# Thirteen weight parts split on other engines, ten of them by GpSimd's scaling and subtraction, with a new order of all jobs and of the memory part's bank reads

## The chip, the cores and the metric

The kernel runs on one core of a Trainium2 chip. The metric is the device time of one execution in microseconds (us), the median of several runs. TensorE (PE) multiplies matrices, VectorE (DVE) and ScalarE (ACT) read its results from PSUM, GpSimd (POOL) works in SBUF alone, and SyncE (SP) issues nearly all DMAs.

## What is computed

The input x has 2048 tokens of 512 numbers. After a layer norm it goes two ways, and the results are added to x:

```python
xn = _layernorm(x)
return x + _A_ref(xn, wq, wk, wv, wo, beta) + _B_ref(xn, w1, b1, w2, b2)

# _A_ref: 32 heads of 16, four segments s of 512 tokens, for each head
p = softmax(q_s @ k_s.T * scale + mask)        # mask adds -1e9 where key > query
a_dot = p @ v_s
a_mem = (phi(q_s) @ M) / (phi(q_s) @ z + 1e-6)
o = g * a_mem + (1 - g) * a_dot                # then o @ wo over all heads
M, z = M + phi(k_s).T @ v_s, z + sum(phi(k_s)) # memory for the next segment

# _B_ref: a second layer norm y of xn, then
h = gelu(y @ w1 + b1)                          # 1792 hidden numbers
out = h @ w2 + b2
```

## The kernel before

**Numbers in two halves.** A float32 operand of a large product is held as two float16 tiles, a high part h and a rest l, and a product takes three matmuls (hh, hl, lh; `split3`, line 482). So every weight matrix is loaded, scaled by a power of two, and split. A matrix is cut into parts (`PARTS`, line 42) and each part into pieces of 128x512. For a part there are loads (`w_load`, SP's DMAs), squares for the scale (`w_square`, line 290; for the parts in `TRACES` four or more small matmuls and a DVE reduction), the scale itself (`w_scale`, line 341: one small matmul job, two ACT and some small DVE instructions), and one split job for each piece (`w_split`, line 364).

**Three ways to split.** The letters of `SPLIT` (line 45) choose one for each piece:

```python
if SPLIT[m][n] == "P":
    G.tensor_scalar(h, r, s, 0.0, op0=OP.mult, op1=OP.add)                 # L371
    V.scalar_tensor_tensor(l, r, s, h, op0=OP.mult, op1=OP.subtract)      # L372
elif SPLIT[m][n] == "V":
    A.activation(h, r, AF.Copy, scale=s)                                   # L374
    V.scalar_tensor_tensor(l, r, s, h, op0=OP.mult, op1=OP.subtract)      # L375
else:                                                                      # "G"
    G.tensor_scalar(r, r, s, 0.0, op0=OP.mult, op1=OP.add)                 # L377
    A.activation(h, r, AF.Copy)                                            # L378
    G.tensor_tensor(l, r, h, op=OP.subtract)                               # L379
```

In all three the three instructions (two for P and V) follow one another.

**Jobs and their order.** The work is cut into 1308 jobs in 41 streams (`streams`, line 55). Attention goes by 16 units i (segment s = i // 4, eight heads each): `T` projects queries (which = 0) or keys (1), sends them to DRAM and fetches them back in another layout (`qk_proj`, line 513; L527 to L529 write, L535 reads), `M` makes scores for the row maxima (`m_jobs`, PE L637, DVE L644), `R` turns the maxima and puts them beside the queries (PE L507, SP L659), `S` makes scores again and takes exponentials (PE L676, ACT L681, POOL L690), `pv` and `PV` multiply with the values (PE L705), `O` normalizes. `N` and `K` update the memory, `Z`, `Qd` and `Q` read it. The MLP goes by 16 half blocks j: `D` (PE L488, DVE L771), `G` (GELU on ACT), `H` (split of the hidden tile by POOL, ACT, POOL) and `e` (PE L812). `V` projects values, `out` the attention result (PE L830). 14 jobs `warm` (`warm_up`, line 838) are fillers: eight matmuls of ones whose result nobody reads.

`ORDER` (line 98) is a string written out by hand or by a planner: each letter names a stream and takes its next job, and that is the order in which every engine's instructions are issued. An engine works through its own instructions strictly in that order. `BANKS` (line 115) gives, in the same order, which of the eight PSUM banks each result takes; a job whose bank is still being read waits on PE. Nothing else sets the order.

**The memory part.** `a_mem` (line 571), part 0, is the job `Qd` of units 4 to 15: two matmuls (PE L579) fill two banks; ACT copies the denominators (L585) and DVE scales the numerators (L588), each from both banks, one half of the partitions from each. In the kernel before ACT begins with the first bank and DVE with the second, and then they change over.

Of the kernel before, what the change touches and what calls it, by code (L numbers as in the profile page):

```python
# [57 lines left out]
def streams():  # L58
# [40 lines left out]
    "aufauucvafauaxuEdwuxEGayFEbayuFGEaaGuAeGzEzFGguHHGJHufFiHAHHhHIJIHpHpJHGIpHJFIppppIjjIBqjBqBgIJKoItIqKKoKujjjCC"  # L99
    "hIKLjqjjLoLoDJKjajrrjnKrrqLrjijtrJjpKpKJLJkrkkpkjrKjrtjkpJpkjrtjKKjltlllpjkrLjkpkjkrjrLLkkgjLllLntqllhppqLrkLDk"  # L100
    "mpupqmkktkmpppjkrrMjjllqlljkrqrjkrrirjkrkjkMarMrjkghpjqrjrajrjqlllnlijrqmqppjjMpqpkjmkpkkjpkjrararmkjrjrrjjtraq"
    "nlallalujrkrrkjrkrbjrarMkappqkjkhqglqlllkkpmpapMkkimppkrkrmjjlllljrjrqkjrrjkrjrkjrkjrMrjkrnkrrqjqjllllMmmogojnm"
    "hsnsoktakkspkqjjkotkjjnlllljjkspqnkkjpkjrkrjrjkrjajllllqrjmrmigprknmhpkkrrtkrkkppnllllnkkrjrnrkrkkpjikpqjjjlltq"
    "llpmpqmpgppjnjqhrqrqrjrrrjrqjrrjjpqpjtrjrjqjrmtpjrnkrkppjkkpkjjpkjaqallllnjakrtrkrarkkrrjakrinrjkrjtllllbarrjam"
    "mpgpkrkrrkmnkkhppknllllnakkupkknpijkkjpqjjlqllljmjojmjgonjjqhqojjmoqjssqjkkskjrkkrrjjrrjtklnlllnkjrrnkjrkrktjrk"
    "rjrkqjrjqjllllsijmqrmpgpkknhkkqpmppkkrpllnllnrjkrjrkjrrkjtritjrkjrrjkpkjrjrqrjqqrjjllllmpnmpgtpjnqhqppppnkrkrrk"
    "rkrrrtakrjrjrqqjarrjrjrjppppmtkjjtqjpppjaaqllllnjjrkqrrkrkaarkrajrirnkrkraallllbrkmrmkgkrkrknkhmpplnlnnllkkpppk"
    "kjpkjkqpjjjlllljqjqoqjjojmjjmgojmnhosnkkkqssnkjksjjklllljrkrjrkrjrkjrkjrkrkrjrjtjrtqqjllllrjrmrmgnhpkpqppnnkkkk"
# [8 lines left out]
    "605426105420416520146502415602415602410526410263502741650713264350174305174304157305417305417340751340751430154"
    "730261275403621750436217450362170362170362170136127306132706312703241567025374167405231670421653704653704653704"
    "653764057364507367540367021365463670241536704521367014352675240136713542067134250675130675301765361075173605361"
    "057317603517670351672504317632054135764021753647021532641253645215364215346213675042103564271063541273065421370"  # L120
    "653470653476053647054367054673056470532617405613247670153026754213064752163045721634514620751342641073526410472"
    "351460723460273436027342607342067342607432607432672017453614270536451270616234561543261542361542361542316542632"
    "154637405216327153406271523147513247513247516324105763245137062451306742513052041352041352054130254130125436026"
    "715430275402631752140635721046213756024137560243561702435726017265410372651403472651304651304651304650134650131"
    "436450173247126503472176350421763504271643276143726143712643712643723164507253106472053161304725163047521463701"
    "643701643701643701734036731430673410675212150627510627615032607"
# [799 lines left out]
```

## Time and profile before

| | us |
|---|---|
| median of 3 runs | 688.02 |
| lowest and highest | 687.28, 688.51 |
| the profiled execution, its own time | 687.96 |
| its span, first to last instruction | 686.3 |

A profile gives each engine's instructions with start and duration. A row of a timeline merges neighbours: start, length, engine, line, operation, tiles, form, count (x12 is twelve instructions), and in brackets the idle time of the engine before it and what ended it. PEld is the weight load that goes beside a matmul; SPq is the issuing of a DMA. Matmuls are pipelined and the ends in the records are modelled, so the length of a merged row is longer than the distance to the next one's start; where a price of a PE job is wanted, that distance is used.

### The profile page before, as it was taken

How to read it: one execution, taken by the hardware profiler on the slowest of the kernel's cores; microseconds unless marked ns; L12 is line 12 of the kernel's file. 1: busy time of each engine (PE TensorE's matmuls, PEld its weight loads, DVE VectorE, ACT ScalarE, POOL GpSimd, SP SyncE). 2: the span in 40 equal slices, each digit the busy share in tenths (PEclk: the TensorE clock that was granted, in tenths of full speed). 3: DMA queues.
4: the chain of work that ended last, by engine and by line, in shares of the span. 5: the costliest groups of instructions: out<-in, count | busy, mean ns of one | idle time of the engine just before them, and what ended most of it. 6: DMA issues, size and time to landing. Idle time of an engine off the chain costs nothing.

```text
span 686.3 us, 17241 instructions
## 1 busy us (share of the span) xinstructions
PE 677.1 (99%) x6465; PEld 389.1 (57%) x6465; DVE 542.6 (79%) x1740; ACT 502.6 (73%) x972; POOL 339.4 (49%) x526
## 2 busy tenths in 40 slices
PE   8999999999999999999999999999999999999997
PEld 6755656565644556565554556557564446556643
DVE  6999977997897867898687886979678697959532
ACT  4585798788785668667796857775875686877970
POOL 4445567446543444564435454445444335565652
PEclk9999999999999999999999999999999999999999
DMA  9886132320305113222123123151020415240101
GB/s 277 258 227 196 47 83 75 94 48 15 112 3 154 32 55 72 65 60 63 58 69 108 34 71 85 32 126 47 17 79 25 116 18 154 33 108 3 19 1 63
DMA packets 52433, 54.89 MB, mean 80 GB/s; under 512 B 5486, under 2 KB 41340, under 8 KB 52348
## 3 DMA queue, kind: packets, MB, share of 16 engines
q1 hardware_dynamic: 50044, 49.59, 25.2%
q0 software_dynamic: 2304, 4.20, 3.8%
q8 instruction: 51, 0.84, 0.5%
q14 instruction: 34, 0.28, 0.1%
HBM read 36.72 MB, written 16.78 MB: 78 GB/s over the span
## 4 chain that ended last, share of the span: by engine, by line
PE 89%; DVE 4%; DMA 3%; ACT 2%; issue 1%; SPq 0%; POOL 0%; ACTq 0%; DVEq 0%
PE ps L488 37%; PE ps L812 20%; PE ps L705 10%; PE ps L830 6%; PE ps L676 5%; PE ps L637 5%; DVE ps L644 2%; PE ps L579 2%; ACT pt L681 1%; PE ps L507 1%; DMA wvs<-in_A_wv_dram 1%; PE ps L843 1%; PE ps L618 1%; PE ps L314 1%; DMA qst<-qd 1%
## 5 line engine op out<-in xcount | busy, mean ns | idle before, releaser
L644 DVE CUSTOM_DVE_ANT_0 ps<-ps,mask 128x512 f32<-128x512 f32 (+3 forms) x512 | 234.2, 523 | 12.9 <-PE ps L637 9.6
L681 ACT ACTIVATE pt<-ps,qkcs 128x512 f32<-128x512 f32 (+1 forms) x384 | 206.8, 625 | 31.8 <-PE ps L676 30.2
L812 PE MATMUL ps<-w2s,hT 64*128 64x512 f16 x1344 | 173.3, 375 | 0.1
L488 PE MATMUL ps<-xnT,w1s 128*128 128x256 f16 x1344 | 157.7, 273 | 0.3
L690 POOL TENSOR_SCALAR_AFFINE_SELECT pt<-pt 128x256 f32<-128x256 f32 x256 | 100.8, 421 | 89.3 <-ACT pt L681 88.1
L488 PEld LDWEIGHTS <-w1s 128*128 128x128 f16 x1344 | 128.0, 98 | 28.3 <-issue 10.3
L787 POOL TENSOR_TENSOR hT<-hh,hT 128x512 f16<-128x512 f32 x64 | 67.5, 1054 | 91.3 <-ACT hT L786 88.3
L812 PEld LDWEIGHTS <-hT 64*128 64x128 f16 x1344 | 68.3, 94 | 56.4 <-issue 2.9
L705 PE MATMUL ps<-pt,vt 128*32 128x512 f32 (+3 forms) x1024 | 76.0, 435 | 0.0
L771 DVE SCALAR_TENSOR_TENSOR hT<-ps,sc,sr 128x256 f32<-128x256 f32 x112 | 51.8, 478 | 24.9 <-PE ps L488 24.0
L644 DVE DVE_READ_ACCUMULATOR2_ANT mc<- 128x1 f32 x512 | 71.4, 139 | 0.1
L676 PE MATMUL ps<-qst,kst 50*128 50x512 f16 (+3 forms) x512 | 63.8, 298 | 0.8 <-ACT pt L681 0.7
L637 PE MATMUL ps<-kst,qst 48*128 48x256 f16 (+3 forms) x512 | 63.0, 297 | 0.5 <-DVE mc L644 0.2
L786 ACT ACTIVATE hT<-hh 128x512 f16<-128x512 f32 x64 | 36.6, 573 | 32.4 <-POOL hh L785 32.1
L705 PEld LDWEIGHTS ps<-pt,vt 128*32 128x32 f32 x1024 | 31.2, 109 | 41.0 <-issue 32.5
L785 POOL TENSOR_SCALAR hh<-hT,sc 128x512 f32<-128x512 f32 x64 | 41.7, 652 | 21.0 <-ACT hT L778 18.6
L778 ACT ACTIVATE hT<-hT,b1t 128x256 f32<-128x256 f32 x112 | 46.7, 496 | 1.1 <-DVE hT L771 0.8
L735 POOL TENSOR_TENSOR nN<-nN,oT 128x512 f32<-128x512 f32 x16 | 20.3, 1271 | 48.4 <-DVE oT L554 48.4
L488 PE MATMUL ps<-xnT,wqs 128*128 128x512 f16 x192 | 44.2, 380 | 0.0
L488 PE MATMUL ps<-xnT,wks 128*128 128x512 f16 x192 | 44.1, 379 | 0.0
L488 PE MATMUL ps<-wvs,xnT 128*128 128x512 f16 x192 | 43.8, 379 | 0.1
L830 PE MATMUL ps<-wos,oT 128*128 128x512 f16 x192 | 43.3, 379 | 0.0
(225 smaller groups left out, 873.5 us busy)
## 6 DMA issues: line engine op xcount, KB each, us to landing
kd<-hl SPq DMA_DIRECT2D x48, 128.0 KB
qd<-hl SPq DMA_DIRECT2D x48, 128.0 KB
kst<-kd SPq DMA_DIRECT2D x32, 192.0 KB
qst<-qd SPq DMA_DIRECT2D x32, 192.0 KB
acc<-in_A_x_dram SPq DMA_DIRECT2D x16, 256.0 KB
acc<-in_B_b_dram POOLq DMA_DIRECT2D x16, 256.0 KB, 4.2
out_dram<-acc SPq DMA_DIRECT2D x16, 256.0 KB
xt<-in_A_x_dram SPq DMA_DIRECT2D x14, 256.0 KB
```

Source lines behind the costliest of these rows:

```text
L488: T.matmul(p, wsl(ws, k, a), xsl(xs, k, b), start=s0 and i == 0, stop=s1 and i == 3 * n - 1)
L637: T.matmul(p[:, o:o + n], stk[i, 0][r, t, P * qb:P * qb + P], stk[i, 1][r, t, :n], start=True, stop=True)
L644: V.tensor_tensor_reduce(p[:, o:o + n], p[:, o:o + n], mask[:, 512 - n:], 1.0, -3e38, OP.add, OP.max, mc[:, 16 * b + 4 * t + qb:16 * b + 4 ...
L676: T.matmul(p[:, o:o + n], stk[i, 1][r, t, P * kb:P * kb + P], stk[i, 0][r, t, P * kb:], start=True, stop=True)
L681: A.activation(e[:, OFF[kbs[0]]:OFF[kbs[0]] + o], p[:, :o], AF.Exp, scale=qkcs[:, 1, i % NG:i % NG + 1])
L690: G.affine_select(v, v, pattern=[[0, 2], [1, P]], compare_op=OP.is_ge, fill=0.0, base=0, channel_multiplier=-1)
L705: T.matmul(p[32 * c:32 * c + 32, P * kb:], vt[s, kb][:, 4 * g + c, 16 * odd:16 * odd + 32], pt[i, 2 * c + odd][:, OFF[kb]:OFF[kb] + LEN[kb ...
L771: V.scalar_tensor_tensor(hz[:, fi, :], p[:, :256], col(F1 + fh), srow[hs][:, own], op0=OP.mult, op1=OP.mult)
L778: A.activation(z, z, AF.Gelu_apprx_tanh, bias=b1t[:, FH * (j % 2) + f:FH * (j % 2) + f + 1])
L787: G.tensor_tensor(hT[:, z, 1, :], t, hT[:, z, 0, :], op=OP.subtract)
L812: w = T.matmul(pes[j][a], hTs[fh][r, fi, u, P * a:P * a + P], w2s[r, fo, v, :], start=n == 0 and m == 0, stop=fi == FH - 1 and m == 2, ski ...
L830: T.matmul(p, o[:, u, P * b:P * b + P], wos[:, g, v, :], start=i == 0, stop=i == 3 * NG - 1)
```

## The change

`SPLIT` changes for 13 pieces of five parts: ten go to G (six from V, four from P), three go from P to V. The order of all 1308 jobs and the bank of each of the 1173 results are new. In `a_mem` both engines now take the first bank, then the second.

```diff
-SPLIT = {"qk": "VV", "QK": "PV", "RK": "PPPP", "v": "VPVP", "1a": "PVPVPVP", "2a": "PVPVPVP", "1b": "GVGVGVG", "2b": "GVGVGVG",
+SPLIT = {"qk": "GV", "QK": "GG", "RK": "PPPP", "v": "GVGP", "1a": "PVGVPGV", "2a": "GVGVPGV", "1b": "GVGVGVG", "2b": "GVGVGVG",
          "o": "GVGV"}
...
 ORDER = (
-    "aufauauucvafauaxuEdwuxEGayFEbayuFGEaaGuAeGzEzFGguHHGJHufFiHAHHhHIJIHpHpJHGIpHJFIppppIjjIBqjBqBgIJKoItIqKKoKujjjCC"
+    "ufucuuaavffxaxawuEdauuyEuGGyEaGzEauzFFaauGFGeAbEGguFHHAGHuIHHHhIJHHppJHJpHIHpppBFpJqIiBjjIIojjIKICtBoKqjjjJgKIh"
...
 BANKS = (
-    "307127514306527014705325621740356523475160172345670124345762013561047235612043715620415642015625401642501654201"
+    "301204250617342570316274261543270437614205043746125036754120637541650237146275031462751462756152746512746512754"
...
-            lo, hi = slice(0, 64), slice(64, 128)
-
-            def den(p, r, z):
+            for b, p in enumerate(ps):
+                r, z = slice(64 * b, 64 * b + 64), slice(64 - 64 * b, 128 - 64 * b)
                 A.activation(rd[r], p[z], AF.Copy, bias=1e-6, scale=qkcs[r, 0, g:g + 1])
-
-            def num(p, r):
                 V.tensor_scalar(n[r], p[r], bg[r, g, 4:5], None, op0=OP.mult)
-
-            den(ps[0], lo, hi)
-            num(ps[1], hi)
-            den(ps[1], hi, lo)
-            num(ps[0], lo)
```

The strings decode to these differences around which the prediction argues. The number in brackets is the job's place in the order, before and after.

```text
fillers                before: 1 4 5 11 14 18 29 36 46 52 105 224 340 693
                       after:  0 2 4 5 16 20 21 24 34 40 50 57 341 700
first traces, before:  warm, k(15), warm, q(20), v0(21), transpose, QK0(24) ... v1(31)
first traces, after:   warm, k(17), warm, warm, q(23), warm, v0(25), v1(26) ... QK0(36)
loads, before:         qk, v0, small, QK, v1, 1a, 1a, RK, 2a, 2a, RK
loads, after:          qk, v0, v1, QK, small, 1a, 1a, 2a, 2a, RK, RK
N of unit 0            before 55 (ahead of the first query projection, 60); after 85 (behind it, 62)
PE between T and M     unit 8:  before 4 D, 5 S, pv to PV, K, N, one filler; after the same without the filler
                       unit 14: before 7 D, 6 S; after 5 D, 4 S, pv to PV
                       unit 15: before 5 D, 4 S, pv to PV; after 5 D, 3 S, pv to PV
PE between R and S     unit 14: before two e, D, T; after PV, D, T
PE between the first   unit 15: before one S, one e; after one S, two e
S and the third S
PE between M and R     unit 15: before pv to PV; after pv to PV and one e
```

The number of changes between jobs that use 128 rows of the array and jobs that use 64 is 210 in both orders, and so is every other count of jobs the same.

## Rows read from the trace of the kernel before

**Rows 1.** The page, part 1: busy time, share of the span, instructions of each engine.
```profile
PE 677.1 (99%) x6465; PEld 389.1 (57%) x6465; DVE 542.6 (79%) x1740; ACT 502.6 (73%) x972; POOL 339.4 (49%) x526
```
**Rows 2.** The page, part 4: chain that ended last, share of the span by engine.
```profile
PE 89%; DVE 4%; DMA 3%; ACT 2%; issue 1%; SPq 0%; POOL 0%; ACTq 0%; DVEq 0%
```
**Rows 3.** Busy time by stretch: length, PE, PEld, DVE, ACT, POOL, PEclk, DMA share, GB/s.
```profile
0.00:60.00 60.00, 56.89 (x469) 39.81 (x471) 50.40 (x178) 37.26 (x76) 24.62 (x42) 1.00 0.86 248
60.00:100.00 40.00, 39.32 (x432) 24.07 (x428) 34.25 (x120) 31.03 (x64) 26.23 (x40) 1.00 0.33 77
100.00:500.00 400.00, 399.47 (x3958) 227.78 (x3955) 327.25 (x1054) 303.45 (x595) 197.84 (x308) 1.00 0.25 66
500.00:686.30 186.30, 181.37 (x1617) 97.42 (x1614) 130.70 (x390) 130.80 (x240) 90.71 (x138) 1.00 0.21 56
```
**Rows 4.** Timeline: PE's first matmul and its last.
```profile
1.60 5.85 PE L843 MATMUL ps<-ones 128*128 128x256 f16 x40 [1.60 <-POOL ones L167]
...
679.70 2.75 PE L830 MATMUL ps<-wos,oT 128*128 128x512 f16 x12
```
**Rows 5.** Timeline: PE (and one weight load) where it waits in the first 25 us.
```profile
8.04 0.41 PE L314 MATMUL ps<-wks 128*128 128x128 bf16 x4 [0.59 <-DMA wks<-in_A_wk_dram]
...
10.40 0.63 PE L314 MATMUL ps<-wvs 128*128 128x128 bf16 x8 [0.85 <-DMA wvs<-in_A_wv_dram]
...
23.35 0.33 PEld L507 LDWEIGHTS ps<-ident,phk 64*128 64x128 f32 x8 [0.34 <-DVE phk L538]
```
**Rows 6.** Timeline: the filler behind 100 us, and the job behind it.
```profile
101.47 1.04 PE L843 MATMUL ps<-ones 128*128 128x256 f16 x8
102.34 1.47 PE L488 MATMUL ps<-xnT,w1s 128*128 128x256 f16 x12
```
**Rows 7.** Split instructions by line: duration min/median/max in ns, first and last start.
```profile
L371 POOL TENSOR_SCALAR w2s<-w2s,sc x4: 692/695/696, 34.1 to 49.8; 128x512 f16<-128x512 f32 x4
...
L371 POOL TENSOR_SCALAR wvs<-pt,sc x1: 1123/1123/1123, 30.0 to 30.0; 128x512 f16<-128x512 f32 x1
...
L374 ACT ACTIVATE w2s<-w2s,sc x5: 707/721/768, 34.1 to 92.2; 128x512 f16<-128x512 f32 x5
...
L375 DVE SCALAR_TENSOR_TENSOR w2s<-w2s,sc x5: 742/744/1085, 39.5 to 94.1; 128x512 f16<-128x512 f32 x5
...
L378 ACT ACTIVATE w1s<-w1s x3: 629/630/630, 59.7 to 73.8; 128x512 f16<-128x512 f32 x3
...
L379 POOL TENSOR_TENSOR w1s<-w1s x3: 1159/1159/1223, 60.4 to 74.5; 128x512 f16<-128x512 f32 x3
```
**Rows 8.** The memory part: ACT's and DVE's copies by line, then ACT's wait: total, times, longest us.
```profile
L585 ACT ACTIVATE rc<-ps,qkcs x24: 679/683/687, 206.8 to 652.2; 64x512 f32<-64x512 f32 x24
...
L588 DVE TENSOR_SCALAR ame<-ps,bg x24: 742/750/759, 207.7 to 652.3; 64x512 f32<-64x512 f32 x24
...
ACT rc L585 <- DVE ame L588: 7.1, 5, 2.3
```
**Rows 9.** Timeline from unit 14's R to unit 15's third S: PE, SP's issue.
```profile
597.82 0.22 PE L507 MATMUL ps<-ident,mc 64*96 64x64 f32 x2
...
598.91 2.47 SPq L659 DMA_DIRECT2D qst<-mhl  x4
...
603.28 0.61 PE L676 MATMUL ps<-qst,kst 50*128 50x512 f16 x6
...
604.73 2.76 PE L488 MATMUL ps<-xnT,wqs 128*128 128x512 f16 x12
...
615.05 2.36 PE L705 MATMUL ps<-pt,vt 128*32 128x512 f32 x32
617.35 0.83 PE L637 MATMUL ps<-kst,qst 48*128 48x512 f16 x2
...
632.95 0.26 PE L507 MATMUL ps<-ident,mc 64*96 64x64 f32 x2 [0.24 <-DVE mc L644]
...
640.23 0.50 PE L676 MATMUL ps<-qst,kst 50*128 50x256 f16 x4 [0.48 <-ACT pt L681]
```

More of the change, by code (lines that the diff above doesn't have):

```diff
@@ L98 @@
 ORDER = (
[L99 to L108, printed above, removed]
@@ L109 @@
-    "ppmpkjjjlltqlljrkrjqrkrtjrkjrkjrkrtjrkrqjrjjltlqllrjrmrpmgkknqhpkkppqkkmppnlllljkjkpjkrktjqrkjrkrjrqjrjrjjrrrrj"
-    "jlllqqljppqmqppkmktrkknrrrkrkpmppqqllllnqrrrrkrrqkkrrrkrqrkrkrnrrllllrrrrrrrrmrrmmrssss"
+    "ufucuuaavffxaxawuEdauuyEuGGyEaGzEauzFFaauGFGeAbEGguFHHAGHuIHHHhIJHHppJHJpHIHpppBFpJqIiBjjIIojjIKICtBoKqjjjJgKIh"
+    "ICjjKqoKJKoDjjLrrjpqnKirjjKrjrKLJpLpJJLqLktkpkrkjrLjrkjrtkrjJrMjjKllKLltlkrpKkjpkjrkLjpktrjLLkgjLLhqpppllllqkDq"
+    "kmppkmkkppkrjrjmjllqllnjkrqrjkrtirktrjkrjarkjrMkaghpjtjrrjqrjllnlqMqlajimrppqmppjkkjpMkkjjqpkjrarmarkrajjrjrqMj"
@@ new lines @@
+    "rnallllaujrkrrkjrbrjaaqrrkkpjkMkhqgqpllllkMkkpmppkmkippkjrmqjjlllljrknrjrakrkrjkrjrkjrkrrjjlMqllljqmjmoonjqmgnh"
+    "ssqskkarkporkqjrkokjjlltlljkjsjkjppkkrjkrrjrtkjrjjlnlllijmpnpmgknhkrrkmrkrrkkppllnllkrtrjkrrkkpkjkqpjjllllnaqmj"
+    "nmigpnjhppqtppmrtqqjjrjrnrrqrrjrjrjrpqpjjqqtrjrjppjrkkrpkjkpjkkqpjaallllnjkrrakrkrakkrrjrjrtkrjjllltlabrjaranip"
+    "mgpmkrkrrknkhkkpplmnnnlllkkppkijkjukjpjkjqlllljqjmjomgojmjnhojjojssqqjnkkskjtrkjrrkjrrjknllnlqljjrkrjkrktrrkjrj"
+    "krrkjjrlllqljiasqmmgpkknhkkppqpkkmpplnlllnjjrkqpkrjrjqrjkrnrkrjjrtkrjrkjrrjjqtllllirqjmrpmgjnhppqnpppprqkrraqrt"
@@ L111 @@
+    "krrkjrtjmkrrkqjrjraqjrrjjrppqptpkjjpppaajltqlllnjrqkjrakrkaarrkrrjkrrikraalllnlbkmgpmkkrkrnkhppklmllnlnpnkrkrkk"
+    "ppjkpjjklqlljjjoqljmqjjomojjqjogjnmhsqnskkkskkskjjltlnlljrkrjrktjrkrkrjrjkrjrkrjrqjjrrjllllqjmqrpmptgkknhpqkkpq"
+    "pkkppmlllnljrkjrjkrjrkjrkjrrjkrjkrjrrjjqltlljrrnjlpqmmgkkrnkhkkkqppmppplllnljkqjtpkrjrkjkrqjkrjrkqjrjjrrrjqjrjl"
+    "lllqrjqpmqpppktkmrrkrkkrrtkpppmqtnlllqlnrrqrkqrrkrkrkqrrrrkrkrrrllnllrrmrrrmrrrrmrrssss"
 )
 BANKS = (
-    "307127514306527014705325621740356523475160172345670124345762013561047235612043715620415642015625401642501654201"
@@ L117 @@
[L117 to L126, printed above, removed]
+    "301204250617342570316274261543270437614205043746125036754120637541650237146275031462751462756152746512746512754"
@@ new lines @@
+    "612754612754617245617245617426157406520363174526103475620156347206723407263406723406723406720374620374620374261"
+    "603745216750432167504321675043125014325014352014305214302513402564317023560247135606213540762135460721360732160"
+    "732163072163072160372160372610732610372612310762301546723401563724150637241560372406372406372406730246734027643"
+    "027634037264306724513067425132510764123570462315704625476025470625470627054627563042156370421673504231670542631"
+    "742631734126374142637142637146243716425043614672503127354601273546307125643170526431720564104237561307425613250"
@@ new lines @@
+    "674135206135206135206513205613205613032561030265147360152314067202531407623106457235107253017215307215307205137"
+    "251030752146302542371754607415607564105176407651024376515024376145023176435716743516741356741356573146573416457"
+    "316457361547307621451206374513260435102674315026740356475120346157207143652071436520736520736052736052730562730"
+    "563201647532015471254630712054637124673162471362471367241236741236172364127364573012474656703124560731245631253"
+    "461253416251634251634235164512316452073631347046137014637014175"
```

## The prediction

> **What bounds the kernel now.** I read the page's first part first. PE is busy 677.1 of 686.3 us, and no other engine is above 79% [rows 1]. The chain that ended last agrees: 89% of it is PE [rows 2]. So 9.2 us of the span are without a matmul, and the stretches say where [rows 3]: 3.1 us before 60 us, 0.7 from 60 to 100, 0.5 from 100 to 500, 4.9 behind 500. Two pieces of it this change cannot touch: the 1.6 us ahead of the first matmul, and the end, 686.3 - (679.70 + 2.75) = 3.85 us for the last addition and store [rows 4]. There remain 9.2 - 1.6 - 3.85 = 3.8 us of idle time. A matmul's record overlaps the next one's, so lateness of less than that overlap shows only as a longer distance between two starts; the reserve is thus above 3.8 us, and I take half as much again, about 6 us, as an estimate.
>
> Both orders hold the same matmuls, the same 14 fillers and as many changes between 128 and 64 rows. PE's work is therefore constant, and the change can only fill waits, or make new ones. DVE looks tight early: 50.4 of the first 60 us [rows 3]. But PE runs at 56.9 there, so a faster DVE pays only where PE waits for it.
>
> **Fillers and loads at the start.** In the first 25 us PE waits 0.59 us for the first key weights, 0.85 us for the first value weights, and 0.34 us for DVE ahead of unit 0's `N` [rows 5]. The new order puts two fillers between the first and second trace and one behind the second, where there was one in all. A filler takes 102.34 - 101.47 = 0.87 us [rows 6]. Two more are 1.74 us, more than the 0.85: that wait goes. `N` moves 30 places, behind the query projection: the 0.34 goes. The 0.59 stays, since five fillers lie ahead of it in both. The fillers come from places 105 and 224, where PE had real work to do (the second is the one at 101.47). What is late next is the trace of the last value weights, now straight behind the first; its two loads move ahead of the second query and key loads on SP's queue, and those and the small loads pass behind it. Loads run at 248 GB/s over these 60 us [rows 3], so its 0.5 MB takes 2.1 us behind the first 0.5 MB, and the two fillers and one trace of eight (a record of 0.63 us [rows 5]) make 2.4 us of cover; with little in hand, a wait of 0 to 0.7 us is possible. Sum of the start: -0.85 - 0.34 = -1.2 us, ends -1.8 (both fillers wholly into waits) and 0 (all of it waited for again). I take -1.2, by that cover.
>
> **The splits.** By [rows 7] P costs POOL 0.70 and DVE 0.74 us; V costs ACT 0.72 and DVE 0.74; G costs POOL 0.70 (the same scaling with another output type), ACT 0.63 and POOL 1.16. The subtraction of P is the same as that of V. Ten pieces to G and three from P to V give:
> - DVE: -10 x 0.74 = -7.4 us.
> - POOL: +6 x 0.70 (from V) + 10 x 1.16 - 3 x 0.70 = +13.7 us, on 24.6 in the first 60 [rows 3]. It fits.
> - ACT: -6 x 0.72 + 10 x 0.63 + 3 x 0.72 = +4.1 us, on 37.3. It fits.
>
> A single split becomes longer: 0.70 + 0.63 + 1.16 = 2.49 us from scale to rest, against 1.46 for V. The new order puts two fillers (1.74 us), the transposes and more between the key scale and the first projection, so I cost this at nothing; without that cover it is 1.0 us once, for the first key piece. The other nine have a projection or more of PE work ahead of their reader. What do DVE's 7.4 us buy? At most the waits that are left around 60 to 100 us: 0.7 visible [rows 3], 1.1 with half as much again hidden. Ends -1.1 and +1.0 (a late split); I take -0.5, because `M`'s and `S`'s banks are read by both DVE and ACT, and ACT gets slower by more than half of what DVE gets faster.
>
> POOL and DVE do not run freely side by side. Most splits on POOL take 0.70 us, but one took 1.12, and of DVE's 0.74 us subtractions one took 1.09 [rows 7]. So a meeting costs 0.35 to 0.43 us. If each of the ten new subtractions meets one, DVE gives back 10 x 0.35 = 3.5 of its 7.4 us. On PE that takes 0.5 us to about 0.25; it does not turn the sign. The Trainium skill, SBUF — State Buffer, section "Who interferes with whom", says that a DVE instruction with two SBUF inputs contends with a GpSimd instruction that reads SBUF, and that the second of the two fully blocks. By that rule alone a meeting could cost up to the other's whole length, 1.16 us, ten times; the rows show the smaller price.
>
> **The memory part.** `Qd` runs 12 times; ACT takes 0.68 us for a bank and DVE 0.75. ACT stood 7.1 us, five times, waiting for DVE's copy of the other bank [rows 8]: each engine ends with the bank the other began with, and the second read waits for the first. In the new form ACT takes both banks without waiting for DVE, and DVE follows it. ACT gains up to 7.1 us over 450 us. Where DVE used to come first (at most the seven other units) it now waits for ACT's first copy, up to 7 x 0.75 = 5.3 us. Neither engine is the bound behind 200 us, and PE idles 0.5 us from 100 to 500 [rows 3]. Net 0, ends -0.4 and +0.4. The Trainium skill, PSUM — Partial Sum Buffer, section "PSUM bank collisions raise a hardware error", would let two engines read different 32-partition quadrants of a bank at once, as these two do. By that rule no wait would be needed in either form and this part is worth nothing; the 7.1 us show that the program orders them all the same.
>
> **The rest of the order.** It is as dense as before, so I look only at distances that shrink. One is the trip of q and k through DRAM between `T` and `M`. Unit 15's `T` ends at 604.73 + 2.76 = 607.49 and `M` starts at 617.35, 9.9 us later, with the records of its two matmuls stretched over 0.83 us where six of an `S` fill 0.61 [rows 9]; so the second half landed late, and the trip takes about 10.1 us. In the new order the work between is shorter by one `S` (0.2 us, a third of that record) at unit 15, by one filler (0.87) at unit 8, and at unit 14 by two `D` and two `S` (2 x 1.47 [rows 6] and 2 x 0.2) against `pv` to `PV` (617.35 - 615.05 = 2.3): 1.0 less. Unit 15 has no slack, so it waits 0.2 + 0.2 = 0.4 us. What slack units 8 and 14 have is not among the rows; I take a third of what they lose, 0.6 for both. Another is `R` to `S` at unit 14: 603.28 - 597.82 = 5.5 us with two `e`, now `PV` in place of them, some 1.0 us less (twelve matmuls of 64 rows against a fourth of that 2.3 us or less). SP ends the issues at 601.38, 1.9 us ahead of `S`, and the landing fills part of that; I take half, +0.5. Sum +1.5. Against it, unit 15's third `S` waited 0.48 and its `R` 0.24 us [rows 9]; each gets one more `e` (six matmuls) ahead of it, so both go, and with them most of the lateness around 617, say 0.5: -1.2. Net +0.3, ends -1.0 and +2.0.
>
> **The sum.** -1.2 - 0.5 + 0 + 0.3 = -1.4 us on the profiled execution's 687.96, so 686.56. The median of the runs, 688.02, is 0.06 above it, and I say **686.5 us**. About 0.2%, 1.4 us, is what a measurement of this kernel can tell from no change (its runs spread over 1.2), so the forecast lies on that line.
>
> **Rivals.**
> 1. *The reserve is really taken.* The start gives 1.8, DVE's relief 1.1, the memory part 0.4, and the new order loses nothing late. -3.3: 684.7 us. For it: all these waits are in the rows. Against: the order before waits at its dense places too, at 617 and 640 us [rows 9]. Chance 0.18.
> 2. *DVE's time is not PE's time.* The start gives 0.6, the splits give nothing, because of meetings with POOL and the longer chain, and new bank waits take the rest: 687.4 us. For it: PE idles just 0.7 us where DVE is fullest. Chance 0.27.
> 3. *Slower, by the trip through DRAM.* It decides once units 8, 14 and 15 and unit 14's `R` to `S` wait for their DMAs more than the 1.7 us that start and splits bring. Without any slack they lose 0.87 + 1.0 + 0.4 + 1.0 = 3.3 us; with trips 0.4 us longer, since ACT and SP are fuller there, 4.5. +4.5 - 1.7 = +2.8: 690.8 us. For it: unit 15 had no slack. Against: PE's idle time from 100 to 500 shows no such wait, so slack is the rule. Chance 0.10.
> 4. *The splits do not relieve DVE at all*, because it waits as long as POOL holds it. At ten times 0.74 us the sum loses its 0.5: 687.0 us, counted with the second.
>
> The forecast has the rest, 0.45, and reaches from 685.6 to 687.4: a little over half of it, 0.28, is faster by over 0.2% (under 686.64), 0.17 within. With the first rival, faster is 0.46. Same is 0.17 + 0.27 and a 0.01 of the third: 0.45; slower 0.09. The range goes from the first rival's time to the second's with 1.5 us more of late waits (the late part's end is 1.7 over what I took): 684.7 to 688.9 us. It leaves out the third rival and half of what lies at the first one's lower side.
>
> **What would show it.** Right: no wait for the value weights near 10 us, all fillers but two before 25 us, DVE 6 to 7.5 us less busy and POOL some 13 more in the first 100 us, ACT's waits for DVE's numerators gone, PE's idle time between its ends near 2.5 us. Wrong: a wait on DMA near 12 us, `M` of units 8, 14, 15 or `S` of unit 14 waiting on a DMA by over 1 us together, or PE's busy time above 678 us, which would mean hidden lateness that these rows do not show.

## The result, and the profile after

The changed kernel takes 690.9 us (690.34 to 691.18, six runs), the kernel before beside it 688.24 (687.28 to 688.51, six runs). The ratio is 1.0043, 95% interval 1.0033 to 1.0053: **slower by 2.7 us** by the medians and 3.0 by the ratio (2.3 to 3.6), where 1.5 us faster was forecast. 690.9 lies outside the range (684.7 to 688.9), and the sign is wrong. The profiled execution took 691.12 us with a span of 689.4.

Inside `a_mem`, L584 is ACT's copy now (L585 before) and L585 DVE's (L588 before). All lines behind `a_mem` are 8 lower: the L629 below is the L637 of before (`M`), L636 is L644, L668 is L676 (`S`), L673 is L681, L697 is L705, L733 is L741, L763 is L771, L777 to L779 are L785 to L787, L787 is L795, L804 is L812, L835 is L843 (the filler). L537 and L538 stand where they stood. Of the runs below, those with the old memory part (1, 3, 9, 15) have the old numbers, and run 8 has 3 more from L733 on.

The page of the changed kernel: part 1, busy time by engine, and the first line of part 4, the chain that ended last beside [rows 1, 2].

```profile
PE 680.1 (99%) x6465; PEld 394.7 (57%) x6465; DVE 542.0 (79%) x1730; ACT 506.1 (73%) x979; POOL 354.1 (51%) x539
...
PE 83%; ACT 5%; DVE 5%; DMA 3%; issue 1%; POOL 1%; SPq 1%; ACTq 0%; DVEq 0%
```

POOL has 14.7 us more and ACT 3.5 more, as worked out (13.7 and 4.1). DVE was to have 7.4 less and has 0.6 less. PE has 3.0 more with the same 6465 matmuls, and its idle time is 9.3 us as against 9.2, so the loss is in its busy time: 1.5 us of that are slower fillers at the start (below), and the rest is lateness that the overlapping records hide. The chain is PE for 83% of the span, where it was 89% [rows 2].

Busy time by stretch, columns and first three stretches as in [rows 3]:

```profile
0.00:60.00 60.00, 57.42 (x461) 40.58 (x462) 47.35 (x168) 36.23 (x75) 36.06 (x53) 1.00 0.81 235
60.00:100.00 40.00, 39.47 (x391) 23.79 (x393) 35.33 (x120) 34.89 (x72) 29.24 (x41) 1.00 0.30 76
100.00:500.00 400.00, 398.81 (x3993) 228.50 (x3986) 326.15 (x1051) 301.80 (x590) 194.84 (x301) 1.00 0.26 68
```

Before 60 us PE idles 2.6 us instead of 3.1. From 100 to 500 it idles 1.2 instead of 0.5. The timeline of PE at the start, where [rows 4, 5] had waits of 0.59, 0.85 and 0.34 us:

```profile
1.60 7.34 PE L835 MATMUL ps<-ones 128*128 128x256 f16 x40 [1.60 <-POOL ones L167]
8.77 0.39 PE L314 MATMUL ps<-wks 128*128 128x128 bf16 x4
...
11.85 0.62 PE L314 MATMUL ps<-wvs 128*128 128x128 bf16 x8
...
26.34 0.63 PE L348 MATMUL ps<-am,ones 128*128 128x1 f32 x4 [0.97 <-DVE am L316]
```

All three old waits are gone (the first only because the fillers ahead of it were slower), and a new one of 0.97 us for DVE's reduction stands at 26 us. The same 40 matmuls of fillers take 7.34 us where they took 5.85, at a granted clock of 1.00 in both; more on that at the end. The timeline 284 to 289 us, PE, DVE and POOL, and last the kernel before's L537 of the same job:

```profile
284.12 0.69 DVE L526 SCALAR_TENSOR_TENSOR hl<-ps,hl 128x512 f16<-128x512 f32 x1
284.41 0.89 POOL L787 DMA_DIRECT2D acc<-in_B_b_dram  x1
284.72 2.72 DVE L537 TENSOR_SCALAR phq<-phq,qksc 128x512 f32<-128x512 f32 x1
...
285.06 1.44 POOL L733 TENSOR_TENSOR oT<-nN,oT 128x512 f16<-128x512 f32 x1
...
286.20 0.96 POOL L777 TENSOR_SCALAR hh<-hT,sc 128x512 f32<-128x512 f32 x1
...
287.19 0.38 PE L629 MATMUL ps<-kst,qst 48*128 48x512 f16 x1
287.48 0.69 DVE L538 SCALAR_TENSOR_TENSOR phq<-ps,phq 128x512 f32<-128x512 f32 x1
...
288.22 0.71 PE L629 MATMUL ps<-kst,qst 48*128 48x512 f16 x2 [0.65 <-DVE phq L538]
```
```profile
288.16 0.48 DVE L537 TENSOR_SCALAR phq<-phq,qksc 128x512 f32<-128x512 f32 x1
```

This is the largest single loss. The second matmul of `M 6 6` needs the bank that `T 7 0` filled and L538 still reads; L538 stands behind L537, and L537, usually 0.48 us, took 2.72 while POOL worked through three instructions without a gap. (The records of L733 and L777, usually 1.16 and 0.69 us, begin while the one before still runs, so they look longer.) `M`'s second matmul comes at 288.22, 1.03 us behind the first, and the four of `M 6 7` behind it, whose banks DVE reads after L538 (L763), lose 0.4 us more. In the order before, `M 6 6` stood ahead of `T 7 0`, and POOL's last part of unit 5's output (L741 there) 30 places later.

L537 as a line, first of the kernel before, then of the changed one, with two other DVE lines of it; times are minimum, median, maximum in ns:

```profile
L537 DVE TENSOR_SCALAR phk<-phk,qksc x12: 471/492/962, 22.1 to 444.6; 128x512 f32<-128x512 f32 x12
L537 DVE TENSOR_SCALAR phq<-phq,qksc x12: 476/478/1400, 169.2 to 610.1; 128x512 f32<-128x512 f32 x12
```
```profile
L537 DVE TENSOR_SCALAR phk<-phk,qksc x12: 476/532/1115, 24.5 to 444.7; 128x512 f32<-128x512 f32 x12
L537 DVE TENSOR_SCALAR phq<-phq,qksc x12: 476/624/2721, 168.8 to 612.7; 128x512 f32<-128x512 f32 x12
...
L538 DVE SCALAR_TENSOR_TENSOR phk<-ps,phk x12: 690/692/692, 25.3 to 445.2; 128x512 f32<-128x512 f32 x12
...
L553 DVE TENSOR_TENSOR oT<-oT,nD x16: 670/691/1481, 106.8 to 671.3; 128x512 f32<-128x512 f32 x16
```

The 24 instructions of this one line sum to 14.7 us before, 18.8 changed (and 17.0 in run 10 below). The splits' subtractions on DVE (L372 and L375) sum to 7.2 us less, nearly the forecast 7.4; L537 alone takes 4.2 of that back; no other line takes back over 0.8. L538, which reads one operand from PSUM, never varies, whatever POOL does beside it; L553, which reads SBUF twice, does.

The memory part's wait, [rows 8]'s 7.1 us of ACT, turned round: now DVE waits, 6.4 us in four times, 1.1 us over the bound of 5.3.

```profile
DVE ame L585 <- ACT rc L584: 6.4, 4, 2.5
```

### The profile page after: what moved, and what is told of

Same layout as the page of the kernel before. It is cut to its first block, busy times and chain, and to the rows that moved or that the text cites. A ratio compares the mean times of both kernels' runs of the same rounds, so it can differ in the third digit from the quotient of the medians.

```text
span 689.4 us, 17230 instructions
## 1 busy us (share of the span) xinstructions
PE 680.1 (99%) x6465; PEld 394.7 (57%) x6465; DVE 542.0 (79%) x1730; ACT 506.1 (73%) x979; POOL 354.1 (51%) x539
## 4 chain that ended last, share of the span: by engine, by line
PE 83%; ACT 5%; DVE 5%; DMA 3%; issue 1%; POOL 1%; SPq 1%; ACTq 0%; DVEq 0%
PE ps L488 35%; PE ps L804 18%; PE ps L697 10%; PE ps L822 6%; PE ps L629 5%; PE ps L668 5%; ACT pt L673 2%; DVE ps L636 2%; PE ps L579 1%; PE ps L507 1%; DMA w2s<-in_B_w_dram 1%; DMA wvs<-in_A_wv_dram 1%; SPq L272 1%; PE ps L610 1%; DVE phq L537 1%
## 5 line engine op out<-in xcount | busy, mean ns | idle before, releaser
L636 DVE CUSTOM_DVE_ANT_0 ps<-ps,mask 128x512 f32<-128x512 f32 (+3 forms) x512 | 234.1, 523 | 15.8 <-PE ps L629 13.4
L673 ACT ACTIVATE pt<-ps,qkcs 128x512 f32<-128x512 f32 (+1 forms) x384 | 207.6, 623 | 33.1 <-PE ps L668 32.4
L804 PE MATMUL ps<-w2s,hT 64*128 64x512 f16 x1344 | 174.9, 375 | 0.1
L779 POOL TENSOR_TENSOR hT<-hh,hT 128x512 f16<-128x512 f32 x64 | 68.2, 1066 | 84.6 <-ACT hT L778 83.1
L804 PEld LDWEIGHTS <-hT 64*128 64x128 f16 x1344 | 73.2, 94 | 50.8 <-issue 3.0
L697 PE MATMUL ps<-pt,vt 128*32 128x512 f32 (+3 forms) x1024 | 76.5, 435 | 0.0
L763 DVE SCALAR_TENSOR_TENSOR hT<-ps,sc,sr 128x256 f32<-128x256 f32 x112 | 52.3, 478 | 29.8 <-PE ps L488 28.9
L636 DVE DVE_READ_ACCUMULATOR2_ANT mc<- 128x1 f32 x512 | 71.1, 139 | 0.1
L629 PE MATMUL ps<-kst,qst 48*128 48x512 f16 (+3 forms) x512 | 65.4, 297 | 0.9 <-DVE phq L538 0.6
L668 PE MATMUL ps<-qst,kst 50*128 50x512 f16 (+3 forms) x512 | 65.3, 298 | 0.6 <-DVE hT L763 0.3
L697 PEld LDWEIGHTS ps<-pt,vt 128*32 128x32 f32 x1024 | 30.3, 109 | 41.7 <-issue 31.4
L777 POOL TENSOR_SCALAR hh<-hT,sc 128x512 f32<-128x512 f32 x64 | 42.0, 656 | 23.1 <-ACT hT L770 21.4
L629 PEld LDWEIGHTS <-qst 48*128 48x128 f16 x512 | 27.3, 94 | 28.4 <-issue 12.5
```

The costliest lines, as they stand in the source:

```text
L629: T.matmul(p[:, o:o + n], stk[i, 0][r, t, P * qb:P * qb + P], stk[i, 1][r, t, :n], start=True, stop=True)
L636: V.tensor_tensor_reduce(p[:, o:o + n], p[:, o:o + n], mask[:, 512 - n:], 1.0, -3e38, OP.add, OP.max, mc[:, 16 * b + 4 * t + qb:16 * b + 4 ...
L668: T.matmul(p[:, o:o + n], stk[i, 1][r, t, P * kb:P * kb + P], stk[i, 0][r, t, P * kb:], start=True, stop=True)
L673: A.activation(e[:, OFF[kbs[0]]:OFF[kbs[0]] + o], p[:, :o], AF.Exp, scale=qkcs[:, 1, i % NG:i % NG + 1])
L697: T.matmul(p[32 * c:32 * c + 32, P * kb:], vt[s, kb][:, 4 * g + c, 16 * odd:16 * odd + 32], pt[i, 2 * c + odd][:, OFF[kb]:OFF[kb] + LEN[kb ...
L763: V.scalar_tensor_tensor(hz[:, fi, :], p[:, :256], col(F1 + fh), srow[hs][:, own], op0=OP.mult, op1=OP.mult)
```

## The experiments

Each run is compared with runs of the kernel before that were made beside it. The changed kernel's 1.0043 is from another such set; the intervals are about 0.001 either way, 0.7 us, so a difference of two ratios is known to about 0.9 us either way.

**Runs 1 to 4: the parts alone.** Run 1 is the kernel before with the new `SPLIT` only, run 2 with the new memory part only, run 3 has the new order and banks with the old splits and memory part, run 4 the new splits and memory part with the new order to place 264 and the old one from there (both orders have done the same jobs at that place).

```diff
-SPLIT = {"qk": "VV", "QK": "PV", "RK": "PPPP", "v": "VPVP", "1a": "PVPVPVP", "2a": "PVPVPVP", ...
+SPLIT = {"qk": "GV", "QK": "GG", "RK": "PPPP", "v": "GVGP", "1a": "PVGVPGV", "2a": "GVGVPGV", ...
```


> The order, the banks and the memory part of the kernel before, with the 13 pieces split as in the changed kernel. Theory A, the loss of 2.7 us is in the new order's own waits: within 0.7 us of the kernel before, since PE has little to win or lose early. Theory B, the splits cost it (POOL 14 us busier, longer chain of one split, meetings with DVE): 1.5 us or more slower. If the relief of DVE were worth what I forecast for it: 0.5 us faster.

Measured: ratio 1.0133 (1.0117 to 1.0149), 8.7 us slower, as theory B has it (1.5 or more). In the old order PE stands 4.88 us at one place for ACT's scale, and the next projection then runs at half pace, 2.4 us longer. Two of ACT's rows show why ACT is late:

```profile
25.71 0.63 ACT L378 ACTIVATE wks<-wks 128x512 f16<-128x512 f32 x1 [4.30 <-POOL wks L377]
...
33.55 0.63 ACT L378 ACTIVATE w1s<-w1s 128x512 f16<-128x512 f32 x1 [2.47 <-POOL w1s L377]
...
43.85 2.75 PE L488 MATMUL ps<-wvs,xnT 128*128 128x512 f16 x12
51.48 5.13 PE L488 MATMUL ps<-wvs,xnT 128*128 128x512 f16 x12 [4.88 <-ACT fa L325]
```
A `G` split puts ACT's copy (L378) between two instructions of POOL, and ACT, which takes its queue in order, stands at five of these copies for POOL's scaling, 12.5 us in all between 21 and 43 us. So its first GELU begins at 44.76 us, where it began at 36.09, and in PE's wait ACT is full (4.37 of 4.40) with what had piled up ahead of the scale. The busy times for 47 to 56.5 us, columns as in [rows 3]:

```profile
47.00:51.40 4.40, 0.00 (x0) 0.00 (x0) 0.70 (x2) 4.37 (x8) 2.49 (x3) 0.79 0.00 1
51.40:56.50 5.10, 5.02 (x13) 1.77 (x13) 3.00 (x10) 3.08 (x7) 1.88 (x2) 0.52 0.79 240
```

The granted clock read 0.79 in the stretch without a matmul, 0.52 (the level of 1.2 GHz) in the one after it, and 1.00 again behind that.

```diff
+            for b, p in enumerate(ps):
+                r, z = slice(64 * b, 64 * b + 64), slice(64 - 64 * b, 128 - 64 * b)
...
-            den(ps[0], lo, hi)
-            num(ps[1], hi)
-            den(ps[1], hi, lo)
-            num(ps[0], lo)
```


> The kernel before with the new bank order of the memory part alone. Theory A: within 0.4 us of the kernel before. Theory C, the memory part costs it (DVE now waits for ACT twelve times, up to 0.75 us each, and holds up banks): 1 us or more slower. ACT's waits for L588, 7.1 us before, fall to near 0 in each theory.

Measured: ratio 1.0012 (1.0003 to 1.0021), 0.7 us slower by medians, between theories A and C. The trace has one new wait of size, and it is again behind an L537: 1.20 us at 367.47 (0.48 in the kernel before), with POOL's subtraction started 0.24 us ahead of it. PE's lateness against the kernel before grows by 0.50 us there.

```profile
367.23 1.16 POOL L779 TENSOR_TENSOR hT<-hh,hT 128x512 f16<-128x512 f32 x1 [0.74 <-ACT hT L778]
367.47 1.20 DVE L537 TENSOR_SCALAR phq<-phq,qksc 128x512 f32<-128x512 f32 x1
...
371.76 0.26 PE L507 MATMUL ps<-ident,mc 64*96 64x64 f32 x2 [0.63 <-DVE mc L636]
```

```diff
-ORDER = ("aufauauucvafauaxuEdwuxEGayFE...
+ORDER = ("ufucuuaavffxaxawuEdauuyEuGGy...
```


> The new order and banks with the old splits and the old memory part. Theory A: 2 us or more slower than the kernel before, with a wait near unit 7's first maxima (about 288 us) only if POOL still holds DVE there. Theory B: within 0.7 us of the kernel before. Theory D, the order was made for the new splits and needs them: slower than the changed kernel, 3.5 us or more above the kernel before, with DVE late before 100 us.

Measured: ratio 1.0165 (1.0149 to 1.0181), 11.5 us slower (theory D's size); PE waits for ACT's exponentials (5.1 us of it), and the three longest of these waits come 5 to 7 us behind a `Qd`. ACT's wait in the old memory part, 7.1 us in [rows 8], is 13.6 in this order:

```profile
ACT rc L585 <- DVE ame L588: 13.6, 9, 2.7
...
PE ps L676 <- ACT pt L681: 3.1, 3, 2.3
PE ps L488 <- ACT pt L681: 2.0, 3, 1.3
```

```diff
-places 0 to 263 of ORDER and BANKS: the order before
+places 0 to 263: the new order; places 264 to 1307: the order before, banks renamed to fit
```


> New splits and memory part; the first 264 jobs in the new order, the rest in the old one (at job 264 both orders have done the same jobs). The two traces stand 0.7 us apart there. Theory A: 0.7 us slower than the kernel before, of which 0.7 us are the slow fillers of the first 9 us if these come again, and 1.1 us a wait for DVE ahead of the scale of part 1a, less what the fillers save. If the loss were spread over all the order: 0.4 us.

Measured: ratio 1.0015 (1.0006 to 1.0024). Run 2, which has the same memory part without the new start, lies at 1.0012: the new start with its splits is worth 0.2 us of loss, within the uncertainty, not the 1.7 us of gain that the prediction had. What follows from the four: splits, memory part and order each lose by themselves, the order and the other two belong together, and no sum of parts predicts the whole.

**Runs 5 to 8: where in the order.** At places 264, 610 and 1083 both orders have done exactly the same jobs. The changed kernel reached them 0.7, 2.1 and 1.9 us later in its trace than the kernel before, and PE's end 3.0 later; the first 0.7 is the key trace, which came at 8.77 us instead of 8.04. Run 5 puts the old order back from 264 to 609, run 6 from 1083 on, run 7 moves the job `par2`, and run 8 leaves out L733 of unit 5, so that half of this unit's output lacks its residual.

```diff
-places 264 to 609 of ORDER and BANKS: the new order
+places 264 to 609: the order before, banks renamed to fit
```


> The changed kernel, but between places 264 and 610 of the order (about 119 to 305 us) the jobs stand as in the kernel before; at both places the two orders have done the same jobs. Theory (the loss comes by stretch, and 1.4 us of it in this one, 1.0 of that because M of unit 6 waits for VectorE's step of the L537 chain): 1.4 us less than the changed kernel, near 689.5, with no wait of M near 288 us. Rival (VectorE and GpSimd meet as often in any order, so the wait only moves): within 0.4 us of the changed kernel.

Measured: 1.0031 (1.0020 to 1.0043), 0.8 us under the changed kernel's ratio, between theory and rival and not clear of no gain (-0.2 to 1.9). `M 6 6` does not wait, but an `S` just behind the seam waits 0.4 us, so this run lacks part of the gain.

```diff
-places 1083 to 1307 of ORDER and BANKS: the new order
+places 1083 to 1307: the order before, banks renamed to fit
```


> The changed kernel, but from place 1083 to the end the jobs stand as in the kernel before. Theory (by stretch): 1.2 us less than the changed kernel, near 689.7, and the many waits of 0.2 to 0.4 us of the matmuls for banks after 480 us fall by about that. Rival (the waits after place 1083 are set by what runs beside them, not by the order): within 0.4 us of the changed kernel.

Measured: 1.0052 (1.0039 to 1.0065), no gain. The wait of 0.29 us at 580 us is gone, but the old order's 0.48 at 640 us [rows 9] is back, and `pv` of unit 12, now straight behind `M`, waits 1.12 us for a bank that DVE still reads. The seam makes its own loss, so this run does not tell what the end costs.

```profile
561.88 1.39 PE L697 MATMUL ps<-pt,vt 128*32 128x512 f32 x12 [1.12 <-DVE mc L636]
```

```diff
-... F a a u G F G e A b E G g u F H H A G H u ...
+... F a a u G F G A b E G g u F H H A G e H u ...
```


> The changed kernel with one job moved: the second parameter step (par2, 4 VectorE instructions and what hangs on them) stands just ahead of part 2 of 1a, where it stood at place 44. Theory (VectorE comes late to the reduction that the matmuls of 1a's fold wait for near 26 us, because par2 and T 0 1 are ahead of it): that wait of 0.97 us falls under 0.4 and the time by 0.6 to 1.0 us, to near 690.1. Rival (the stall is only handed on, since PE waits next for the splits or the loads): no wait there, and another of the same size before 60 us; time within 0.2 us.

Measured: 1.0046 (1.0033 to 1.0059); the rival holds. The wait at 26 us is gone, and one of 1.15 us for the same line's reduction stands at 24, in front of the moved job's own matmul:

```profile
23.82 0.23 PE L847 MATMUL ps<-ident,mhl 14*128 14x14 f32 x1 [1.15 <-DVE am L316]
```

```diff
-            G.tensor_tensor(t[:, 1, :], n, t[:, 0, :], op=OP.subtract)
+            if i == 5:
+                A.activation(t[:, 1, :], n, AF.Copy)
+            else:
+                G.tensor_tensor(t[:, 1, :], n, t[:, 0, :], op=OP.subtract)
```


> The changed kernel, but the last subtraction of unit 5's output (L733, GpSimd, 1.44 us at 285 us) is left out: ScalarE writes a plain copy in its place, so that half of that unit's output holds a copy and not the residual. Nothing else differs. Theory (VectorE's L537 of 0.47 us took 2.72 because GpSimd's instructions stood back to back beside it): L537 near 284.7 takes at most 1.6 us, M of unit 6 at 288.2 no longer waits 1.0 us, and the time falls by 0.6 to 1.2 us. Rival 1 (L537 is slow for a reason of its own, or GpSimd's next instruction takes the place): L537 stays over 2 us and the time within 0.3. Rival 2: L537 falls, but the matmuls wait for something else by then, time within 0.3.

Measured: 1.0022 (1.0013 to 1.0031), 1.4 us under the changed kernel's ratio (0.5 to 2.4). L537 of `T 7 0` falls from 2.72 to 0.83 us, and `M 6 6` no longer waits:

```profile
283.78 0.89 POOL L790 DMA_DIRECT2D acc<-in_B_b_dram  x1
284.09 0.83 DVE L537 TENSOR_SCALAR phq<-phq,qksc 128x512 f32<-128x512 f32 x1
...
284.45 1.01 POOL L780 TENSOR_SCALAR hh<-hT,sc 128x512 f32<-128x512 f32 x1
...
286.57 0.60 PE L629 MATMUL ps<-kst,qst 48*128 48x512 f16 x6
```

**Runs 9 to 12: the terms, and joining what paid.** Run 9 has the two fillers of the prediction's first term alone: `N` and the loads stay where they were, and a filler stands ahead of `N`.

```diff
-place 105: filler; place 224: filler
+ahead of the first value trace (place 21): filler; ahead of N 0 (place 55): filler
```


> The kernel before with nothing changed but two of its 14 fillers: the ones at places 105 and 224 stand ahead of the first value trace (place 21) and ahead of N of unit 0 (place 55), where TensorE waits 0.85 and 0.34 us. It is the prediction's first term alone. Theory (that term holds, and the changed kernel loses it again elsewhere): 0.8 to 1.2 us faster than before, near 686.5. Rival (a filler of 0.87 us in a wait pushes back the work behind it as much as it frees later, or the waits that the fillers filled at places 105 and 224 come back): within 0.4 us of before.

Measured: 1.0007 (0.9998 to 1.0016); the rival holds. Both waits are gone, but the first query projection starts at 25.97 us where it started at 24.43. Of these 1.54 us, 0.75 are the key trace that came later (8.79 against 8.04); the rest is two fillers of 0.87 us in waits of which, with the keys that late, only a part was left. And at its old place a filler covered a wait: the first job behind 100 us was followed after 1.33 us by the filler and after 2.20 by the next job [rows 6 show the last two]; without the filler the next job follows after 1.73 us and waits, so 0.47 us come back of 0.87.

```profile
100.41 1.48 PE L488 MATMUL ps<-xnT,w1s 128*128 128x256 f16 x12
102.14 1.47 PE L488 MATMUL ps<-xnT,w1s 128*128 128x256 f16 x12 [0.24 <-ACT pt L681]
```

Run 10 is the changed kernel with nothing but one job moved, the last part of unit 5's output:

```diff
-O 5 2, e 5 0, A 6 0, H 5 2, H 5 3, M 6 6, M 6 7, e 5 1, M 6 8
+e 5 0, A 6 0, H 5 2, H 5 3, M 6 6, M 6 7, e 5 1, O 5 2, M 6 8
```


> The changed kernel with one job moved by some eight places and nothing left out: the last part of unit 5's output (L732 on ScalarE and L733 on GpSimd) stands behind M 6 7, ahead of M 6 8. Theory (back-to-back GpSimd work beside L537 is what M 6 6 waits for): as in the run that left L733 out, 1.0 to 1.4 us less than the changed kernel, ratio to before near 1.0022. Rival (GpSimd's subtraction comes to lie beside another instruction of the same kind and costs as much there): within 0.4 us of the changed kernel.

Measured: **1.0013 (1.0004 to 1.0021)**. From 1.0043 that is 0.0030, with the two intervals together 0.0013 either way: 2.1 of the 3.0 us, 1.2 to 3.0, more than the 1.0 to 1.4 expected. PE's end comes 3.1 us sooner in the trace: 1.6 of it between 286 and 290 us, 1.0 at `M 6 6`'s second matmul and the rest at `M 6 7`; and 1.4 because the fillers at the start ran faster in this execution (key trace at 7.39 instead of 8.77), though both kernels have the same jobs there. The traces of runs 8, 13 and 14, which have no L537 of 2.72 us either, show the same 1.6 us at this place.

```profile
283.01 0.89 POOL L787 DMA_DIRECT2D acc<-in_B_b_dram  x1
283.32 0.83 DVE L537 TENSOR_SCALAR phq<-phq,qksc 128x512 f32<-128x512 f32 x1
```

Run 11 adds the old end to it, run 12 also the old start with the two fillers early.

```diff
+ahead of place 1083 as run 10; from there the order before, with M 13 11 behind PV 12 1
```


> The same, and from place 1083 to the end the jobs in the order of the kernel before, with M 13 11 moved behind PV 12 1, because with that order's end alone it waited 1.4 us. Theory (about 1.2 us of the loss is in the end's many small waits): 0.8 to 1.2 us less than the run with unit 5's part moved, ratio near 1.0007. Rival (the small waits come in any order): within 0.4 us of it.

Measured: 1.0038 (1.0024 to 1.0052): `pv` and `R` behind the seam wait 1.42 and 1.51 us for DVE. That is 1.7 us more than run 10, where the rival had no change and the theory a gain.

```diff
+places 0 to 263: the order before and the old SPLIT, fillers as in run 9; from 264 as run 11
```


> Everything that paid: the order of the kernel before to place 264 with the two fillers early and the old splits, the new order from 264 to 1083 with unit 5's part moved, the end of the kernel before with M 13 11 moved, and the new memory part. Theory (the terms add up): the run before's ratio less the 0.8 to 1.2 us of the fillers and 0.2 of the old start: 0.3 to 1.0 us faster than the kernel before. Rival (joining pieces makes new waits of its own, as it did twice): as slow as before or up to 1 us slower.

Measured: 1.0053 (1.0041 to 1.0066), 3.6 us slower than before, where even the rival had at most 1: the waits of run 11, and 1.05 us for the second key weights at 12 us. No version beats the kernel before.

**Runs 13 to 15: the rest, and a counter-test.** Run 13 is run 10 with the second trace of 2a ahead of 1a's fold; run 14 takes two more small waits away.

```diff
-wf 1a, ws 1a 0, ws 1a 1, T 0 0, wm 2a 1
+wm 2a 1, wf 1a, ws 1a 0, ws 1a 1, T 0 0
```


> The changed kernel with unit 5's part moved (as in the run before), and one job more: the second trace of 2a's weights (0.8 us of TensorE's work) stands ahead of 1a's fold, where TensorE waits 1.0 us for VectorE's reduction. Theory (this wait, which the new start put in the place of the two it removed, is most of the 0.9 us that are left): 0.6 to 0.9 us less than with unit 5's part alone, ratio near 1.0002. Rival (handed on, as when the parameter step was moved: the fold comes later and the first hidden stage waits for its weights): within 0.3 us of it.

Measured: 1.0014 (1.0003 to 1.0025), as run 10. The wait is handed to the job put in its place, which waits for a reduction of the same line:

```profile
25.75 0.96 PE L314 MATMUL ps<-w2s 128*128 128x128 bf16 x14 [1.22 <-DVE am L316]
```

```diff
-D 1 3 in bank 5, S 0 0 2 in banks 1 and 2; S 13 2 1, S 13 2 2, D 13 5
+D 1 3 in bank 1, S 0 0 2 in banks 5 and 2; D 13 5, S 13 2 1, S 13 2 2
```


> The same, and two small waits taken away: D 1 3 and the S after it exchange banks (0.6 us of waiting for ScalarE at 70 us), and D 13 5 stands ahead of the S that waits 0.3 us at 577 us. Theory (the rest of the loss is such single waits, each of which can be moved into work that is there): 0.5 to 0.9 us less than the run with 2a's trace, and so at or under the kernel before. Rival (a wait so removed comes back within the next few jobs): within 0.3 us of it.

Measured: 1.0023 (1.0013 to 1.0033). Both waits are gone, others, 0.7 us at 73 and 0.5 at 587, are new. The rival holds in run 13; in run 14 its mechanism shows, and the time is 0.6 us above run 13's, which the two intervals do not tell from none.

Run 15 plants the meeting in the kernel before.

```diff
-H 5 2, T 7 0, ... M 6 6 (place 568), O 5 2 (place 600)
+H 5 2, O 5 2, T 7 0, e 5 0, H 5 3, e 5 1, G 6, M 6 6 in T 7 0's bank
```


> The kernel before with the suspected meeting planted: the last part of unit 5's output (L740 on ScalarE, L741 on GpSimd) moved from place 600 to just ahead of T 7 0, and M 6 6 moved behind T 7 0 into its bank. Theory: L537 of T 7 0, 0.48 us near 288 us, takes 1.2 to 2.7 us, M 6 6 or the job behind it waits 0.3 to 1.1 us, and the kernel is 0.3 to 1.5 us slower than before. Rival (L537 is only slow where something else of the new order holds VectorE): L537 stays under 0.8 us and the time within 0.4 us.

Measured: 1.0050 (1.0034 to 1.0066), more than expected, but not by the meeting: L537 kept its 0.48 us.

```profile
286.40 1.15 POOL L741 TENSOR_TENSOR oT<-nN,oT 128x512 f16<-128x512 f32 x1
...
287.42 0.48 DVE L537 TENSOR_SCALAR phq<-phq,qksc 128x512 f32<-128x512 f32 x1
287.53 0.71 POOL L785 TENSOR_SCALAR hh<-hT,sc 128x256 f32<-128x256 f32 x1
...
288.68 0.39 PE L637 MATMUL ps<-kst,qst 48*128 48x512 f16 x2 [2.46 <-DVE phq L538]
```

L741 had 0.13 us left when L537 began, so they all but missed each other. `M` waited 2.46 us because I left two jobs between it and `T`; behind a `T` its bank is read by L522, L525, L526 and L538 in turn, with L537, which works in SBUF, ahead of the last. The planting failed as a test of the meeting. What it shows is the other half of the mechanism: a job in `T`'s bank so soon behind it waits even without a meeting.

## Why the prediction was wrong

Forecast and measurement are 4.4 us apart (-1.4 and +3.0). Taking runs 2 and 4 as parts of a sum, which they are only roughly, 1.9 us of that lie in the start with its splits (-1.7 forecast, +0.2 measured), 0.8 in the memory part and 1.6 in the rest of the order (+0.3 forecast, +1.9 measured), each known to about 0.9 us.

**The failed step that made the kernel slower is "The rest of the order"**: "It is as dense as before, so I look only at distances that shrink", net +0.3, and in it only distances through DRAM and from `R` to `S`. The largest loss came from a pair of queues that this step never laid side by side: POOL's instructions against DVE's, at 284 us, where neither engine's work had changed, only the order. Runs 8 and 10, which change one POOL instruction's engine or place, take back 1.4 and 2.1 of the 3.0 us, and the traces of four runs show 1.6 us at that place. The distances that the step did look at cost nothing: units 14 and 15 do not wait at `M`, nor unit 14 at `S`, and at unit 15, which was to wait 0.4 us more, the 0.44 us of waiting before are gone.

**The price in "The splits" failed with it.** "So a meeting costs 0.35 to 0.43 us", and "the rows show the smaller price": these were two meetings with only 0.56 and 0.54 us left of the other instruction. In this study's 17 profiles L537 ran 408 times. In 394 its length is, within 0.06 us, 0.48 us, or what is left of POOL's running instruction plus 0.28, whichever is more; in 168 of these it was held. Two rows of the changed kernel: 1.27 - 0.44 + 0.28 = 1.11, and 1.16 - 0.04 + 0.28 = 1.40.

```profile
407.85 1.27 POOL L727 TENSOR_TENSOR nN<-nN,oT 128x512 f32<-128x512 f32 x1 [3.18 <-DVE oT L554]
408.29 1.11 DVE L537 TENSOR_SCALAR phk<-phk,qksc 128x512 f32<-128x512 f32 x1
...
448.55 1.16 POOL L779 TENSOR_TENSOR hT<-hh,hT 128x512 f16<-128x512 f32 x1 [1.62 <-ACT hT L778]
448.59 1.40 DVE L537 TENSOR_SCALAR phq<-phq,qksc 128x512 f32<-128x512 f32 x1
```
Where L537 starts first, POOL waits instead. From the kernel before, a subtraction of usually 1.16 us:

```profile
171.82 0.48 DVE L537 TENSOR_SCALAR phk<-phk,qksc 128x512 f32<-128x512 f32 x1
171.88 1.43 POOL L787 TENSOR_TENSOR hT<-hh,hT 128x512 f16<-128x512 f32 x1 [0.74 <-ACT hT L786]
```
So a meeting is a full block of the second by the first, and the rows of before held its price (L537's maximum of 1400 ns) on a line that I did not look at. (The 0.28 can be L537's own work once POOL has ended; no run tells that from a handover.) The Trainium skill says of such a meeting that the second fully blocks (SBUF — State Buffer, section "Who interferes with whom"). The same section names `tensor_scalar` among the operations that can take the shared pair of ports; L537 is one. I used the section's sentence on two SBUF inputs for ten new subtractions only. It is in three profiles (the changed kernel and runs 6 and 7) that L537 reached 2.72 us: what was left of a DMA issue (0.58), the whole of L733 (1.16), the whole of L777 (0.69) and 0.28 make 2.71. The other 11 misfits are 0.70 us beside two of POOL's selects.

**Fillers and loads at the start, -1.2: wrong.** The waits of 0.85 and 0.34 us went as said, and no time came of it: run 9 gives +0.5 us (-0.1 to 1.1), run 4 less run 2 gives +0.2. In run 9 the two fillers pushed back what stands behind them, and their old places gave back less than they cost. "All fillers but two before 25 us" held, and the wait moved to DVE's reduction at 26 us, which runs 7 and 13 could only hand on.

**The splits, -0.5: the sums right, the effect not there.** DVE's subtractions gave 7.2 us, POOL and ACT took what was said. PE got nothing: L537 took 4.2 of it, and in the old order the longer chain through ACT costs 8.7 us (run 1). The forecast's "without that cover it is 1.0 us once" saw one late split. Run 1, which takes the new order away, shows the longer chain as a late queue: ACT waits in it for POOL five times, and everything behind in ACT's queue comes late too, at over eight times the size.

**The memory part, 0 with ends of 0.4:** run 2 measured +0.7 (0.2 to 1.4), above the upper end by its middle. ACT's wait went and DVE's came, as said; what the trace shows of the loss is one more L537 that now meets POOL (0.50 us).

**The rivals.** The third named 690.8, and 690.9 was measured, but for another reason, so the agreement is luck. PE's waits of 0.2 us and more name DVE, ACT and the first constant, and no DMA; of the trips through DRAM only unit 8's shows, 0.16 us between the first two matmuls of its `M`, where the kernel before has 0.33.

The second rival and its "meetings with POOL" had the mechanism, at 687.4 us: it let them eat the gain and not more. Of the signs listed, "PE's busy time above 678 us, which would mean hidden lateness" came true with 680.1, though 1.5 us of it are the slower first fillers and not hidden lateness.

**Open:** the last 0.9 us (0.3 to 1.4) of run 10. Start, end and single waits were each tried (runs 6, 7, 11, 13, 14), and each wait taken away came back within a few jobs; no one place holds it. In run 15 the planted meeting did not come about, so the mechanism is shown by taking meetings away (runs 8 and 10) and by the lengths, not by making one. What makes POOL's next instruction go ahead of a waiting L537 in one case and not in another (run 8's stood through one only) was not tried.
